# The last row of w_down in nine transfers in place of one

## The chip, the cores and the metric

The kernel runs on one core of a Trainium2 chip. The metric is the device time of one execution in microseconds. Lower is better. Before the change the median of three runs is 409.6 us (409.38 to 409.67).

## The reference

One decoding step of a transformer block, one token with a hidden size of 1024, everything in bfloat16:

```python
h  = x + attention(layernorm(x), k_cache, v_cache, wq, wo)   # 32 query heads, 4 KV heads, 65536 cached positions, head size 128
h2 = h + (gelu(n @ w_gate) * (n @ w_up)) @ w_down            # n = layernorm(h), 3584 inner columns
```

The two caches are 64 MB each, the five weight matrices together some 39 MB. All of it is read once, so the program is a stream out of HBM with the arithmetic laid alongside.

## The kernel before, in words

A ring in SBUF takes the stream in pieces. First come the two halves of wq, then for each of eight steps (a KV head and a half of the positions) the keys and the values, then wo, w_gate, w_up and w_down. Nearly all loads are issued by SyncE on one hardware queue, in the order in which they are used, each as soon as its place in the ring is free. A class `Flow` writes out this order up to w_up with semaphores set by hand (its instructions all carry line 105); TensorE's part of the attention is a loop.

For the end of the program w_down (3584 x 1024) is cut by rows. Two pieces lie in the ring: `wa` has 16 weight rows for each of the 128 partitions, `wb` 8. The last four rows of each partition lie in a tensor of their own, `w_end` (128 x 4 x 1024), so that they need not wait for room. Here "row" has two meanings: a row of w_down, of 1,024 numbers and 2 KB, and the position e that it has in its partition. One position over 128 partitions is 128 rows of w_down, 256 KB.

Behind a barrier (line 568) SyncE issues four loads, the list `loads` (line 576): `wa`, `wb`, positions 0 to 2 of `w_end`, position 3 of `w_end`. Each has a semaphore of its own, `end_sem[i]`, which counts up by 16 when the whole transfer has landed (line 579 and the lines behind it). They are issued right after one another, around 377 to 379 us, while the load of w_up still runs, and stand in the queue behind it. They take part in no wait that the framework would add; TensorE waits for the semaphores itself.

TensorE's order at the end is written by hand too. When w_up has landed, it multiplies with it (line 626); DVE and ScalarE bring the inner columns into `actz`. Then TensorE waits for `wa`, multiplies its 16 positions by wide matmuls (`down_wide`, line 647), and folds the sum into the output's banks (`add_wide`, line 653). Then comes the loop at lines 664 to 668: for each of the other three loads it waits for the load's semaphore and does `down` for each of its positions, eight matmuls of 128 columns (line 634): 8 positions of `wb`, three of `w_end`, and the last of `w_end`. Two casts (DVE, line 670; ScalarE, line 671) round the sum, and SyncE stores 2 KB (line 672).

So the last transfer has 128 pieces of 2 KB, one for each partition, and what comes behind its landing is eight matmuls, a cast, and the store.

Of the kernel before, what the change touches and what calls it, by code (L numbers as in the profile page):

```python
# [118 lines left out]
def kernel(  # L119
# [13 lines left out]
    nc = tc.nc  # L133
    P = 128
# [80 lines left out]
    end_sem = [tc.alloc_semaphore("end_landed_%d" % i) for i in range(4)]  # L215
# [40 lines left out]
    def select(key, out, op_, fill, base, pattern, mult, rows=None):  # L256
# [14 lines left out]
       in_=ident_f[:].rearrange("p (q m) -> p q m", q=4).unsqueeze(2).to_broadcast([P, 4, NI, SQ]))  # L271
# [285 lines left out]
    def ffn_load(wmat, s0):  # L557
        rk = ["R%d" % s0, "R%d" % (s0 + 1)]
        wv = slot(s0, 2)[:, 0:DC * F].rearrange("p (c n) -> p c n", c=DC)
        f.dma("sp", wv, wmat.rearrange("(p c) n -> p c n", p=P), w=rk, sem=r_sem[s0], wait=[(s_step, STEPS * NT2 - 1)])  # L560
        return wv, rk
# [5 lines left out]
    up_w, _ = ffn_load(B_w_up, 2)  # L567
    with tc.tile_critical(no_gpsimd_drain=True):  # L568
# [6 lines left out]
    FM = FB - FZ  # L575
    loads = [(wa, B_w_down[0:P * FA, :].rearrange("(p e) n -> p e n", p=P)), (wb[:, 0:FM, :], wb_src[:, 0:FM, :]),
             (w_end[:, 0:FZ - 1, :], wb_src[:, FM:FB - 1, :]), (w_end[:, FZ - 1:FZ, :], wb_src[:, FB - 1:FB, :])]
    for (dst, src), sem in zip(loads, end_sem):
        d = nc.sync.dma_start(out=dst, in_=src)  # L579
        d.then_inc(sem, 16)  # L580
        tc.no_tile_sem_insts.add(d.ins.name)
        tc.add_to_no_dep_group("loads", d.ins)
        tc.keep_in_program_order(d)
    waits_itself = nc.tensor.nop()
    tc.declare_fence(waits_itself.ins, group="loads")

# [44 lines left out]
    def down(a_row, w_row):  # L631
        for j in (0, 4, 1, 5, 2, 6, 3, 7):
            q, m = divmod(orow[j], 32)
            nc.tensor.matmul((d_ps, d_odd)[q // 2][32 * q:32 * q + 32, :], lhsT=a_row[:, AZ - m:AZ - m + 32], rhs=w_row[:, j * OB:(j + 1) * OB],  # L634
                             start=False, stop=False, skip_group_check=True, tile_position=(0, 32 * q))
# [25 lines left out]
    stay_busy(2)  # L661
    add_wide()
    e = FA
    for (dst, _), sem in list(zip(loads, end_sem))[1:]:
        nc.tensor.wait_ge(sem, 16)
        for i in range(dst.shape[1]):
            down(actz[:, e, :], dst[:, i, :])
            e += 1
# [34 lines left out]
```

## Time and profile before

| | |
|---|---|
| median of the runs | 409.6 us |
| time of the profiled execution | 409.33 us |
| its span, first to last instruction | 407.6 us |
| DMA queue of SyncE and its loads, share of 16 engines | 98.5% |
| mean rate of the DMA engines | 425 GB/s |
| TensorE, DVE, ScalarE busy | 57%, 49%, 10% |
| issue of the last load | 378.77 us |
| its landing | 404.72 us |
| issue of the store | 405.46 us |

The share of busy time is over the whole span. The end is read from stretches of a few tenths of a microsecond: there the DMA share, times 16, is the number of DMA engines that still move data.

The names in the views: `ring<-in_B_w_down_dram` are the loads `wa` and `wb`, `w_end<-in_B_w_down_dram` the two loads of `w_end`. "SPq" is SyncE's queue of issues. In a line of the timeline stand the start, the time from the first to the last of the group, the engine, line and operation, the number of instructions, and in brackets the idle time before the group with what ended it. In a line of stretches stand the stretch and its length, the busy time of TensorE, its weight loads, DVE, ScalarE and GpSimd (with the number of instructions), the granted clock of TensorE, the DMA share and the rate in GB/s.

### The profile page before, as it was taken

The page shows a single profiled execution, that of the slowest core. Times are in us where ns is not written, and L with a number is a line of the kernel's source. Part 1 is how long each engine was busy: PE and PEld are TensorE (multiplying, and loading weights), DVE is VectorE, ACT ScalarE, POOL GpSimd, SP SyncE. Part 2 cuts the span into 40 slices and gives each one's busy share as a digit, 9 for nine tenths or more (in the row PEclk, how much of TensorE's full clock was granted, in tenths as well). Part 3 has the DMA queues.
Part 4 walks back from the last instruction along what each step waited for, and adds up shares of the span by engine and source line. Part 5 has one row for each costly group of instructions (what it writes and reads, how often), then busy time and mean ns, then how long its engine had stood idle before and what let it go on. Part 6 is the DMA issues. An engine that isn't in the chain of part 4 may idle for free. (4 is left out here: it accounts for less than half of the span.)

```text
span 407.6 us, 3706 instructions
## 1 busy us (share of the span) xinstructions
PE 231.4 (57%) x1556; PEld 102.6 (25%) x1557; DVE 200.8 (49%) x160; ACT 40.0 (10%) x142; POOL 16.7 (4%) x27
## 2 busy tenths in 40 slices
PE   0432854584577368717971785468466746625366
PEld 0110322231232133203321332223123223222323
DVE  2226860875089328734763686089508940110310
ACT  1000003000300220030003000300030013000000
POOL 4210000001000000010000001000000000000200
PEclk9955996799589778976796889589956986865668
DMA  8999999999999999999998999999999999999995
GB/s 360 412 447 426 428 447 412 460 418 421 445 460 418 412 432 482 418 412 418 482 431 386 444 424 447 418 466 412 415 450 466 418 408 418 464 445 429 402 412 224
DMA packets 4958, 173.10 MB, mean 425 GB/s; under 512 B 596, under 2 KB 600, under 8 KB 856
## 3 DMA queue, kind: packets, MB, share of 16 engines
q1 hardware_dynamic: 4904, 173.02, 98.5%
q8 instruction: 4, 0.07, 0.1%
q14 instruction: 2, 0.02, 0.0%
q10 hardware_dynamic: 48, 0.00, 0.0%
HBM read 173.02 MB, written 0.00 MB: 424 GB/s over the span
## 5 line engine op out<-in xcount | busy, mean ns | idle before, releaser
L105 DVE STREAM_TRANSPOSE ktb<-ring 128x4096 f32<-128x4096 f32 x32 | 141.1, 4417 | 73.9 <-DMA ring<-in_A_k_cache_dram 73.9
L450 PE MATMUL bank<-ktb,qs 128*128 128x512 bf16 x512 | 131.4, 416 | 53.5 <-PEq L436 53.5
L450 PEld LDWEIGHTS bank<-ktb,qs 128*128 128x128 bf16 x512 | 51.4, 103 | 130.3 <-issue 84.1
L462 PE MATMUL bank<-ring,pt 128*32 128x512 bf16 x512 | 44.3, 522 | 36.6 <-PEq L436 36.6
L105 ACT ACTIVATE pt<-sc,nb 128x256 bf16<-128x256 f32 x64 | 31.5, 494 | 257.6 <-DVE nb L105 257.6
L105 DVE STREAM_TRANSPOSE sc<-bank 128x512 f32<-128x512 f32 x32 | 22.2, 695 | 37.8 <-PE bank L450 37.8
L462 PEld LDWEIGHTS bank<-ring,pt 128*32 128x32 bf16 x512 | 18.7, 126 | 59.0 <-issue 55.1
L105 PE MATMUL bank<-ring,xz 128*32 128x512 bf16 (+1 forms) x128 | 13.2, 598 | 16.8 <-DMA ring<-in_B_w_gate_dram 9.9
L105 DVE TENSOR_REDUCE mx<-sc 128x8 f32<-128x2048 f32 x8 | 18.3, 2286 | 0.3
L454 PE MATMUL bank<-ident_f,mx 128*8 128x128 f32 x8 | 2.7, 333 | 25.8 <-PEq L436 25.8
L105 POOL COPY qs<-qsel 128x512 bf16<-128x512 bf16 x4 | 5.3, 1326 | 232.7 <-PE bank L450 218.7
L105 ACT ACTIVATION_READ_ACCUMULATOR pt<-sc,nb 128x1 f32 x64 | 12.0, 187 | 0.0
L471 PE MATMUL bank<-sel,acc_sb 128*128 128x8 f32 x64 | 8.2, 255 | 6.2 <-PEq L436 6.2
L105 PEld LDWEIGHTS bank<-ring,xz 128*32 128x32 bf16 x128 | 4.8, 139 | 23.8 <-issue 14.9
L471 PEld LDWEIGHTS bank<-sel,acc_sb 128*128 128x128 f32 x64 | 7.7, 191 | 10.0 <-issue 10.0
L105 ACT COPY acc_sb<-bank 128x512 f32<-128x512 f32 x8 | 4.7, 585 | 47.0 <-PE bank L462 47.0
L626 PE MATMUL bank<-ring,xz 128*32 128x512 bf16 (+1 forms) x64 | 5.8, 556 | 4.9 <-PEq L621 4.9
L454 PEld LDWEIGHTS bank<-ident_f,mx 128*8 128x8 f32 x8 | 0.7, 83 | 29.5 <-issue 29.5
L607 DVE MEMSET bank<- 128x128 f32 x1 | 0.2, 165 | 15.2 <-SPq L568 15.2
L603 DVE STREAM_TRANSPOSE ktb<-bank 128x512 f32<-128x512 f32 (+1 forms) x4 | 2.3, 618 | 10.3 <-PE bank L626 10.3
L456 PE MATMUL bank<-diag,ones_f 8*128 8x8 f32 x16 | 3.9, 312 | 5.7 <-PEq L436 5.7
L105 DVE STREAM_TRANSPOSE ktb<-bank 128x512 f32<-128x512 f32 x2 | 1.4, 716 | 11.2 <-PE bank L105 11.1
(101 smaller groups left out, 76.5 us busy)
## 6 DMA issues: line engine op xcount, KB each, us to landing
ring<-in_A_k_cache_dram SPq DMA_DIRECT2D x16, 4096.0 KB, 24.8
ring<-in_A_wq_dram SPq DMA_DIRECT2D x2, 4096.0 KB, 16.6
ring<-in_A_wo_dram SPq DMA_DIRECT2D x2, 4096.0 KB, 24.1
ring<-in_B_w_gate_dram SPq DMA_DIRECT2D x1, 7168.0 KB, 26.1
ring<-in_B_w_up_dram SPq DMA_DIRECT2D x1, 7168.0 KB, 31.8
ring<-in_B_w_down_dram SPq DMA_DIRECT2D x1, 4096.0 KB, 20.2
ring<-in_B_w_down_dram SPq DMA_DIRECT2D x1, 2048.0 KB, 24.7
w_end<-in_B_w_down_dram SPq DMA_DIRECT2D x1, 768.0 KB, 25.8
```

What stands on the lines that cost most here:

```text
L105: ins = getattr(self.eng[e], o["call"])(**o["kw"])
L450: m = nc.tensor.matmul(bank[c][:], lhsT=qs[:, jt].rearrange("p s c -> p (s c)")[:, s * P:(s + 1) * P], rhs=mv[:, :, J, :, u], start=(s == ...
L454: nc.tensor.transpose(out=mxT_ps, in_=mx1[:], identity=ident_f[:]).then_inc(s_step, 1)
L456: nc.tensor.matmul(bc_ps, lhsT=ones_f[0:rep, :], rhs=diag[:], start=True, stop=True).then_inc(s_step, 1)
L462: m = nc.tensor.matmul(acc[32 * q:32 * q + 32, :], lhsT=pt[:, c, n, :, :].rearrange("p h s -> p (h s)"), rhs=v_sb[:, c, :, n, :], start=(c ...
L471: m = nc.tensor.matmul(o_ps, lhsT=acc_sb[:, u * Dh:(u + 1) * Dh], rhs=sel[:, u:SQ:NS], start=(u == 0), stop=(u == NS - 1))
L603: nc.vector.transpose(out=r[:, o:o + n].rearrange("p (e j) -> p e j", j=32), in_=ps.rearrange("p (j e) -> p e j", j=32))
L607: nc.vector.memset(d_ps, 0.0)
L626: nc.tensor.matmul(f_banks[t // 4][32 * q:32 * q + 32, :], lhsT=hz[:, ci, :], rhs=w, start=(ci == 0), stop=(ci == DC - 1), tile_position=( ...
```

## The change

The last load, position 3 of `w_end`, is issued as nine transfers by partitions: the first 64, then 1, 3, 5, 7, 9, 11, 13 and 15. Together they are the same 128 pieces of 2 KB from the same places to the same places. All nine count up the same semaphore, and TensorE waits for 9 x 16 = 144 in place of 16. The other three loads, their order and the matmuls stay.

```diff
-    for (dst, src), sem in zip(loads, end_sem):
-        d = nc.sync.dma_start(out=dst, in_=src)
-        d.then_inc(sem, 16)
-        tc.no_tile_sem_insts.add(d.ins.name)
-        tc.add_to_no_dep_group("loads", d.ins)
-        tc.keep_in_program_order(d)
+    stairs, p0 = [], 0
+    for n in [P // 2] + list(range(1, 16, 2)):
+        stairs.append(slice(p0, p0 + n))
+        p0 += n
+    assert p0 == P
+    shares = [[slice(0, P)]] * 3 + [stairs]
+    for (dst, src), sem, share in zip(loads, end_sem, shares):
+        for p in share:
+            d = nc.sync.dma_start(out=dst[p], in_=src[p])
+            d.then_inc(sem, 16)
+            tc.no_tile_sem_insts.add(d.ins.name)
+            tc.add_to_no_dep_group("loads", d.ins)
+            tc.keep_in_program_order(d)
...
-    for (dst, _), sem in list(zip(loads, end_sem))[1:]:
-        nc.tensor.wait_ge(sem, 16)
+    for (dst, _), sem, share in list(zip(loads, end_sem, shares))[1:]:
+        nc.tensor.wait_ge(sem, 16 * len(share))
         for i in range(dst.shape[1]):
```

## The prediction

> **What bounds the kernel now.** I read the page first: the slices and the queues of its parts 2 and 3, then the chain that ended last, then stretches of the last microseconds, the timeline there, and the waits of SyncE.
>
> ```profile
> DMA  8999999999999999999998999999999999999995
> DMA packets 4958, 173.10 MB, mean 425 GB/s; under 512 B 596, under 2 KB 600, under 8 KB 856
> q1 hardware_dynamic: 4904, 173.02, 98.5%
> q8 instruction: 4, 0.07, 0.1%
> q14 instruction: 2, 0.02, 0.0%
> ```
>
> The 16 DMA engines are busy from the first slice to the last but one, 98.5% of the span with loads alone: the kernel is a stream of 173 MB, and it ends when the last byte of w_down is in and used. Programs are fetched through the same engines (q8, q14).
>
> ```profile
> 378.77 25.95 DMA w_end<-in_B_w_down_dram
> 404.72 0.04 issue
> 404.76 0.35 PE bank L634 x8
> 405.12 0.02 issue
> 405.14 0.26 ACT h L671
> ```
>
> The chain in order of time (start, duration): the transfer that the change cuts up is the last load on it. Its issue is at 378.77, but it stands in the queue for most of its 25.95 us; what sets the end is when the slowest engine finishes its part.
>
> ```profile
> 401.60:401.80 0.20, 0.20 (x4) 0.20 (x6) 0.00 (x0) 0.00 (x0) 0.00 (x0) 1.00 1.05 430
> 402.60:402.80 0.20, 0.20 (x28) 0.20 (x20) 0.00 (x0) 0.00 (x0) 0.00 (x0) 1.00 0.56 205
> 403.20:403.40 0.20, 0.18 (x16) 0.00 (x1) 0.00 (x0) 0.00 (x0) 0.00 (x0) 1.00 0.23 92
> 403.60:403.80 0.20, 0.00 (x0) 0.00 (x0) 0.00 (x0) 0.00 (x0) 0.00 (x0) 1.00 0.25 92
> 404.00:404.20 0.20, 0.06 (x4) 0.06 (x8) 0.00 (x0) 0.00 (x0) 0.00 (x0) 1.00 0.16 61
> ```
>
> Stretches of 0.2 us (engines' busy time, granted clock, DMA share, GB/s). The DMA share falls from 1.05 to 0.23: from 403.2 on, about four of sixteen engines still work. The stream doesn't end at once; it drains over two microseconds.
>
> ```profile
> 404.14 0.34 PEld L634 LDWEIGHTS <-ktb 128*32 128x32 bf16 x24 [0.94 <-DMA w_end<-in_B_w_down_dram]
> 404.76 0.12 PEld L634 LDWEIGHTS <-ktb 128*32 128x32 bf16 x8 [0.28 <-DMA w_end<-in_B_w_down_dram]
> SPq L672 <- DVE h L670: 26.2, 1, 26.2
> ```
>
> TensorE multiplies the three rows of the third transfer at 404.14, stands idle for 0.28 us, and takes the last row. SyncE, which issues the loads, has nothing else for 26.2 us.
>
> **Which engines are late.** The trace has every DMA packet's start and duration. On each engine a packet starts where the one before ended, so they fall into sixteen chains, all of which process the same sequence. Behind the first to finish, the sixteen end the last transfer at 0, 0.12, 0.26, 0.27, 0.29, 0.31, 0.35, 0.37, 0.45, 0.49, and then 0.93, 1.37, 1.69, 1.84, 1.96 and 1.98 us. The lags are old: they stay for hundreds of microseconds, since no engine ever runs dry. Each of the six late ones got its lag at a program fetch on that engine: 16,384 bytes at 31.9, 353.9, 376.9 and 401.0 us cost some 1.5 us each, 8,192 bytes at 103.2 and 144.3 us 1.0 and 0.7. The records do not give an engine's number.
>
> **The change, part by part.**
>
> *The shares.* Now every engine has 8 packets of 2,048 bytes in the last transfer, 80 ns each by the records, 0.64 us, and one 6 ns mark that counts up the semaphore. After: 64 rows over sixteen engines, 4 packets each; then eight transfers of 1 to 15 rows. How many engines a small transfer uses is shown twice: the x load of 32 rows left two packets and a mark on each of sixteen, and the output store of 4 rows left 4 packets and 4 marks. I take the nearest, the store: n rows, n engines, one packet each. If the eight always begin at the same engine, the shares are 12, 11, 11, 10, 10, 9, 9, 8, 8, 7, 7, 6, 6, 5, 5 and 4 packets (sum 128, as before), with up to 8 further marks: from +0.32 + 0.05 = +0.37 us for the first engine to -0.32 us for the last. If they rotate, each keeps 8 packets, +0.02 us on average for marks. The Trainium skill, "DMA: Bandwidth & Descriptors", section "Why a DMA increments its semaphore by 16 and not by 1", says that a transfer takes the largest count up to 16 that divides its rows, on the lowest-numbered engines. By that rule the shares are the graded ones; the store's four marks agree, and no row shows an odd count.
>
> *Which shares the late engines get.* This is what decides, and nothing in the trace tells. Bounds: all three of the latest (1.84, 1.96, 1.98) at the light end, where the end would come up to 0.3 us sooner, or the latest on the first engine, +0.37. Each of the sixteen orders being as likely, I drew the sixteen shares at random over the sixteen lags: the latest of lag plus share is in the middle +0.17 us, one time in ten below -0.01, one in ten above +0.35, and only one time in ten is it a gain. That is because three engines lie within 0.15 us, two packets, and the worst share among them counts. The ten early engines have 1.49 us (1.98 - 0.49) to spare, more than any share takes. I take +0.17.
>
> *What a gain is cut by.* If the last row lands sooner, TensorE is still at the three rows before it, which come over the same late engines and are not changed. The 0.28 us of idle time in the row above is all that can be had.
>
> *Issues.* SyncE issues twelve loads in place of four. The two issues to w_end took 0.43 us each, so eight more are 8 x 0.43 = 3.4 us: from 379.2 to 382.6. The first of these rows is wanted by the engines at some 402.4, 20 us later, and behind them on SyncE is only the store at 405.46, under the 26.2 us. Costed at nothing; were the cover gone it would be 3.4 us. No other engine waits for SyncE after its barrier at 377.1, and nothing on ACT's queue or POOL's is moved.
>
> *The wait.* TensorE's wait is for 144 in place of 16, still one instruction. Behind it are the last 8 matmuls, then the two casts and the store, as before: 0.
>
> *TensorE's work* is the same 96 matmuls on the same tiles: 0.
>
> Sum, against the profiled execution's own time of 409.33 us (span 407.6 and 1.7 outside): 409.33 + 0.17 = 409.5. The median of the runs is 409.6, 0.27 above that execution, so 409.6 + 0.17 = 409.8.
>
> **The rivals.**
>
> *Light shares for the late engines.* Were the late engines late because they stand at the end that the small transfers skip, the gain is 0.15 to 0.28 us: 409.3 to 409.5. For it: four of the six carry the same kind of fetch, so they may be neighbours. Against it: neighbours in the middle or at the front are as likely.
>
> *Writers in each other's way.* Today every transfer of the stream goes to all 128 rows at once, and the steady 80 ns shows no conflict. Now sixteen engines write within the first 64 rows, and then within the last 64; if two that share a way into SBUF halve their rate, the packets of the late four go from 80 to up to 160 ns. Over 8 packets that is +0.64, with the +0.17 some +0.3 to +0.85 us: 409.9 to 410.45. Against it: when the late four drain, the other twelve are done, and the four are 0.3 us apart. The Trainium skill, "SBUF — State Buffer", section "Door 1: The DMA port swizzle", has 64 adjoining rows on only 8 of 16 ports, which speaks against this change; no run here shows it, and by it the sum would be this rival's.
>
> *A fetch more.* Eight more instructions may push SyncE's program over the edge of a block. The 8 KB fetches cost their engine 0.7 and 1.0 us; it counts in full only on one of the three latest: 410.3 to 410.6. Against it: ten of sixteen engines have 1.49 us to spare.
>
> *Slower: the odd transfers go to one engine.* If a count that isn't a power of two isn't spread, one engine has 4 + 64 = 68 packets in place of 8: 60 x 0.08 = 4.8 us more. On an engine as late as the latest the end moves by 4.8, on the earliest by 4.8 - 1.98 = 2.8: 412.4 to 414.4. It decides from 25 packets (1.98 / 0.08) on an early engine, from any on a late one. For it: no row shows an odd count; the rows shown are 128, 32 and 4. Against it: the 4.
>
> **How the numbers follow.** Forecast 0.62; light shares 0.12; writers in the way 0.12, a third of which passes 0.2%; a fetch 0.04, half of it; one engine 0.08; 0.02 for what I have not seen, put to faster. 0.2% (0.8 us) is about what a measurement of this kernel can tell from no change; no share of the staircase moves it by that. Same: 0.62 + 0.12 + 0.08 + 0.02 = 0.84; slower 0.04 + 0.02 + 0.08 = 0.14; faster 0.02. The range goes from 409.3 (light shares in full) to 410.5 (writers in the way), leaving the one-engine case and part of the fetch out, 0.1 to 0.15 in all.
>
> **What would show it.** The queue's packet count should rise by 8 transfers' marks, 64, the bytes staying. Stretches of 0.2 us from 402.4 should show the early ten engines drain more unevenly and about four busy up to 404.2. The landing of the last of w_end at 404.6 to 405.1, and TensorE's idle time before its last 8 matmuls between 0 and 0.65 us in place of 0.28. SyncE: twelve issues, the last ended near 382.6. Wrong would be: a long single-engine tail (DMA share 0.06 for microseconds), packets of 2 KB well over 80 ns, a third q14 packet, or lags that don't come from the fetches.

## The result and the profile after

The changed kernel takes 410.39 us (median of ten runs, 410.29 to 410.79), beside 409.40 us for the kernel before. The ratio is 1.0024, with a 95% interval of 1.0015 to 1.0034: a loss of about 1.0 us. The profiled execution took 410.39 us, with a span of 408.7.

The page of the changed kernel, its slices and queues:

```profile
DMA  8999999999999999999999998999999999999994
DMA packets 5022, 173.10 MB, mean 424 GB/s; under 512 B 660, under 2 KB 664, under 8 KB 920
q1 hardware_dynamic: 4968, 173.02, 98.4%
q8 instruction: 4, 0.07, 0.1%
q14 instruction: 2, 0.02, 0.0%
```

The stream is the same 173.10 MB with 64 packets more, the marks of the eight added transfers (a mark is the 4-byte packet by which an engine counts up the semaphore; a transfer of n rows left n of them, and 1 + 3 + ... + 15 is 64). No program fetch was added. The chain that ended last, in order of time:

```profile
381.60 0.35 SPq L586
381.94 0.04 issue
381.98 23.81 DMA w_end<-in_B_w_down_dram
405.79 0.04 issue
405.83 0.35 PE bank L641 x8
406.19 0.02 issue
406.21 0.26 ACT h L678
```

The landing moved from 404.72 to 405.79, +1.07 us, and what comes behind it is as before: 0.04, 0.35, 0.02. (The first line is the eleventh of twelve issues; the twelfth starts at 381.98, where the DMA line starts, and ends at 382.35.) So the whole loss lies ahead of the landing. Some stretches ahead of it, the first from the kernel before, the others from the changed one (stretch, length, busy times of the engines, clock, DMA share, GB/s):

```profile
402.40:402.60 0.20, 0.20 (x23) 0.20 (x24) 0.00 (x0) 0.00 (x0) 0.00 (x0) 1.00 0.81 318
```

```profile
402.40:402.60 0.20, 0.20 (x20) 0.20 (x24) 0.00 (x0) 0.00 (x0) 0.00 (x0) 1.00 0.89 184
402.60:402.80 0.20, 0.20 (x29) 0.20 (x21) 0.00 (x0) 0.00 (x0) 0.00 (x0) 1.00 0.82 164
...
404.60:404.80 0.20, 0.00 (x0) 0.00 (x0) 0.00 (x0) 0.00 (x0) 0.00 (x0) 1.00 0.09 31
404.80:405.00 0.20, 0.02 (x4) 0.03 (x7) 0.00 (x0) 0.00 (x0) 0.00 (x0) 1.00 0.00 0
405.00:406.00 1.00, 0.66 (x32) 0.44 (x32) 0.00 (x0) 0.00 (x0) 0.00 (x0) 1.00 0.00 0
```

Two things are to be seen. From 402.4 to 402.8 more engines are busy than before and move less; in the first of these stretches a busy engine moves about half as much: 318 / (0.81 x 16) = 24.5 GB/s before, 184 / (0.89 x 16) = 12.9 after. And from 404.8 no DMA engine has anything to do, but the transfer lands at 405.79, one microsecond later. TensorE's timeline shows the same gaps:

```profile
404.98 0.34 PEld L641 LDWEIGHTS <-ktb 128*32 128x32 bf16 x24 [1.73 <-DMA w_end<-in_B_w_down_dram]
405.83 0.12 PEld L641 LDWEIGHTS <-ktb 128*32 128x32 bf16 x8 [0.51 <-DMA w_end<-in_B_w_down_dram]
```

The three positions of the third transfer come 0.84 us later than before (404.14), though that transfer wasn't changed, and the last position waits 0.51 us in place of 0.28.

The records of single packets tell where. Of two late engines in the changed kernel (bytes of a packet and its duration in ns, M where a mark was written, in us):

```
6144:239 6144:234 6144:234 6144:324 6144:452 6144:475 6144:258 6144:234 M404.007
   2048:84 x4 M404.332  2048:84 M404.418  2048:84 M404.504  2048:84 M404.590
   2048:84 M404.676  2048:84 M404.762
... 6144:351 6144:412 6144:292 6144:432 6144:339 6144:275 M404.391
   2048:86 2048:85 2048:84 2048:84 M404.721  2048:84 M404.807
```

Their 6 KB packets took 235 ns before and up to 475 now, while the early engines were at their single rows, whose 2 KB packets took mostly 110 to 175 ns. The last packet of all ended at 404.81, in the kernel before at 404.29: +0.52 us. And the six marks that the first of these engines wrote 86 ns apart, from 404.332 on, reached the semaphore at 404.811, 405.007, 405.203, 405.399, 405.595 and 405.791: 196 ns apart. (The records of landings don't name the engine; these six are taken for its marks by their number and their even steps, here and below.) So from the last packet to the landing it is 0.98 us, in place of 0.43: +0.55. Together +1.07.

Two theories came out of this, beside that of the prediction (graded shares): **conflict** of engines that write a few adjoining rows at once, and **late marks**, an engine's marks passing one after another at a fixed pace. A string of marks is such a row: each is written before the one ahead of it has landed.

### The profile page after: what moved, and what is told of

Its sections match the earlier page's. It is cut to its first block, busy times and chain, and to the rows that moved or that the text cites. A ratio compares the mean times of both kernels' runs of the same rounds, so it can differ in the third digit from the quotient of the medians.

```text
span 408.7 us, 3714 instructions
## 1 busy us (share of the span) xinstructions
PE 227.1 (56%) x1556; PEld 101.6 (25%) x1557; DVE 200.8 (49%) x160; ACT 40.0 (10%) x142; POOL 16.7 (4%) x27
## 2 busy tenths in 40 slices
DMA packets 5022, 173.10 MB, mean 424 GB/s; under 512 B 660, under 2 KB 664, under 8 KB 920
## 5 line engine op out<-in xcount | busy, mean ns | idle before, releaser
L462 PE MATMUL bank<-ring,pt 128*32 128x512 bf16 x512 | 42.4, 504 | 36.5 <-PEq L436 36.5
L105 PE MATMUL bank<-ring,ktb 128*32 128x512 bf16 x64 | 6.1, 545 | 2.7 <-DMA ring<-in_A_wo_dram 2.0
```

Source lines behind the costliest of these rows:

```text
L105: ins = getattr(self.eng[e], o["call"])(**o["kw"])
L462: m = nc.tensor.matmul(acc[32 * q:32 * q + 32, :], lhsT=pt[:, c, n, :, :].rearrange("p h s -> p (h s)"), rhs=v_sb[:, c, :, n, :], start=(c ...
```

## The experiments

Each is compared with the kernel before on the same chip, whose median there was 409.34 us (two halves, 8 tiny on one semaphore, 64 rows last, eight of 16) or 409.35 us (the other four). Each edit is against the changed kernel.

| kernel | us | ratio, 95% interval | last packet ended | landing | between |
|---|---|---|---|---|---|
| before | 409.4 | | 404.29 | 404.72 | 0.43 |
| the change | 410.39 | 1.0024 (1.0015 to 1.0034) | 404.81 | 405.79 | 0.98 |
| two halves | 410.0 | 1.0015 (1.0006 to 1.0024) | 404.91 | 405.32 | 0.41 |
| even and odd rows | 409.39 | 1.0001 (0.9992 to 1.001) | 404.18 | 404.59 | 0.41 |
| uncut, 4 tiny behind | 409.99 | 1.0018 (1.0009 to 1.0027) | 404.36 | 405.34 | 0.98 |
| uncut, 8 tiny behind | 410.68 | 1.003 (1.0019 to 1.0041) | 404.44 | 406.09 | 1.65 |
| the same, own semaphores | 410.94 | 1.0038 (1.0024 to 1.0051) | 404.52 | 406.25 | 1.73 |
| 64 rows last | 410.49 | 1.0027 (1.0017 to 1.0038) | 404.87 | 405.90 | 1.03 |
| eight of 16 adjoining rows | 410.79 | 1.0035 (1.0021 to 1.0049) | 404.87 | 406.08 | 1.21 |
| the change, rows spread | 410.25 | 1.002 (1.0011 to 1.0029) | 404.29 | 405.43 | 1.14 |

(The last three columns are from one profiled execution of each: the packet and semaphore records. "Last packet" includes its mark.)

**Two halves.**

```diff
-    stairs, p0 = [], 0
...
+    stairs = [slice(0, P // 2), slice(P // 2, P)]
```

> The last load as two transfers, the first 64 rows and the last 64: equal shares of 8 packets on every engine, two marks per engine with 4 packets between them. Before: 409.4 us, the change: 410.4. If the loss comes from many engines writing within half of the rows, most of the conflict is here too: the late engines' 6,144-byte packets go from 235 to 280 to 480 ns, and the time to 409.9 to 410.1. If the conflict needs transfers of a few adjoining rows, packets stay at 84 and 235 ns and the time within 0.1 us of before. If the loss comes from strings of marks, 409.4: two marks 0.33 us apart make no string. If it comes from graded shares, 409.4.

410.0 us: 0.66 us lost with equal shares and without a string of marks. The stretch and the landing of this kernel:

```profile
402.40:402.60 0.20, 0.20 (x20) 0.20 (x24) 0.00 (x0) 0.00 (x0) 0.00 (x0) 1.00 0.89 174
...
404.80:405.00 0.20, 0.17 (x12) 0.17 (x16) 0.00 (x0) 0.00 (x0) 0.00 (x0) 1.00 0.03 10
```

```profile
404.83 0.35 PEld L637 LDWEIGHTS <-ktb 128*32 128x32 bf16 x24 [1.61 <-DMA w_end<-in_B_w_down_dram]
405.36 0.12 PEld L637 LDWEIGHTS <-ktb 128*32 128x32 bf16 x8 [0.19 <-DMA w_end<-in_B_w_down_dram]
```

The busy engines are as slow as in the change (174 GB/s at a share of 0.89), and the bytes end 0.62 us late; the landing follows them by 0.41 as before. In the records the late engines' 6 KB packets go up to 489 ns, and the early engines' second four packets of 2 KB take 124 to 207 ns. Their first four stay at 84. So there is a loss with lengthened packets and without a string of marks, at the size that the first case named; that it comes from the place of the rows, and not from having two transfers, is for the next run to show.

**Even and odd rows**, the same two transfers with other rows.

```diff
+    stairs = [slice(0, P, 2), slice(1, P, 2)]
```

> The last load as two transfers of 64 rows again, but the even rows and then the odd rows in place of the first half and the second. Count of transfers, shares and marks are those of the two adjoining halves (410.0 us beside 409.34 before). If the loss there comes from where the rows lie, every packet stays at 84 and 235 ns here, and the time is 409.3 to 409.5. If it comes from having two transfers on the same tensor in flight, or from the second mark, 410.0 again.

409.39 us, ratio 1.0001.

```profile
402.40:402.60 0.20, 0.20 (x28) 0.20 (x20) 0.00 (x0) 0.00 (x0) 0.00 (x0) 1.00 0.69 256
```

```profile
404.63 0.12 PEld L637 LDWEIGHTS <-ktb 128*32 128x32 bf16 x8 [0.28 <-DMA w_end<-in_B_w_down_dram]
```

A busy engine moves 23 GB/s here (256 / 11.0), every packet of the late engines stays at 84 and 234 ns, but for the two at a program fetch, of 654 and 369 ns (as before), and the idle time before the last eight matmuls is the 0.28 us of the kernel before. Where the rows lie is the whole of the 0.66 us; a second transfer and a second mark cost nothing that can be measured. The Trainium skill, "SBUF — State Buffer", section "Door 1: The DMA port swizzle", has 64 adjoining rows on 8 of 16 ports, and by its formula the even rows are on all of them; this pair of runs agrees, 410.0 beside 409.39 us. But the even and odd rows lie elsewhere in HBM too, so the runs don't tell whether it is the writes to SBUF or the reads from HBM that get in each other's way; that it is the writes is argued, from the ports that the Trainium skill gives, and not shown.

**Eight tiny transfers behind an uncut last load.**

```diff
+    stairs = [slice(0, P)]
...
+    for i in range(NTINY):   # 8
+        d = nc.sync.dma_start(out=tiny[:, i, :], in_=B_w_down[i, 0:512].rearrange("(p n) -> p n", p=16))
+        d.then_inc(end_sem[3], 16)
...
-        nc.tensor.wait_ge(sem, 16 * len(share))
+        nc.tensor.wait_ge(sem, 16 * (len(share) + (NTINY if sem is end_sem[3] else 0)))
```

> The last load stays one transfer of 128 rows, and eight transfers of 16 pieces of 64 bytes are issued behind it on the same semaphore, so that every engine has nine marks in place of one and hardly more bytes (8 x 64 B, some 17 ns for a piece and its mark). If an engine's marks reach the semaphore only some 0.2 us after one another, however fast they are written, the landing comes 8 x 0.18 = 1.4 us later, with no DMA packet running in that time: 410.8 to 411.0. If marks cost what the packet records show (6 to 9 ns), 8 x 0.02 = 0.16 us: 409.6. The conflict of writers and the graded shares have no part in this kernel: 409.6 by them.

410.68 us, just under what late marks were given. The stretches and TensorE's timeline:

```profile
404.40:404.60 0.20, 0.20 (x24) 0.11 (x9) 0.00 (x0) 0.00 (x0) 0.00 (x0) 1.00 0.02 1
404.60:404.80 0.20, 0.09 (x8) 0.00 (x0) 0.00 (x0) 0.00 (x0) 0.00 (x0) 1.00 0.00 0
404.80:405.00 0.20, 0.00 (x0) 0.00 (x0) 0.00 (x0) 0.00 (x0) 0.00 (x0) 1.00 0.00 0
405.00:406.00 1.00, 0.00 (x0) 0.00 (x0) 0.00 (x0) 0.00 (x0) 0.00 (x0) 1.00 0.00 0
```

```profile
404.17 0.52 PE L645 MATMUL bank<-w_end,ktb 128*32 128x128 bf16 x24 [0.78 <-DMA w_end<-in_B_w_down_dram]
406.13 0.30 PE L645 MATMUL bank<-w_end,ktb 128*32 128x128 bf16 x8 [1.44 <-DMA tiny<-in_B_w_down_dram]
```

Nothing runs on the whole core for over a microsecond: the bytes are there, the third transfer came as early as before, and TensorE waits 1.44 us for marks alone. In the packet records a piece of 64 bytes and its mark take 13 ns; in the time it is 1.34 / 8 = 0.17 us each. That is an average: the last landings are a string of nine, from 404.521 to 406.089, each 0.196 us behind the one before, as in the change. Other strings of nine in this trace have steps of 0.151, 0.159, 0.177 and 0.203 us, each nearly the same from mark to mark. Late marks are shown without conflict: no packet is lengthened, but for the two at a program fetch.

**Four of them.**

```diff
-    NTINY = 8
+    NTINY = 4
```

> As the kernel with eight tiny transfers behind an uncut last load, with four of them. If marks pass one after another at a fixed pace, the loss is half: 1.34 / 2 = 0.67 us, 410.0, with the landing 0.17 to 0.2 us later for each. If the loss is a fixed price for having tiny transfers there, 410.7 again.

409.99 us, 0.64 us lost: half, as a fixed pace has it, 0.16 us each.

```profile
405.38 0.30 PE L645 MATMUL bank<-w_end,ktb 128*32 128x128 bf16 x8 [0.72 <-DMA tiny<-in_B_w_down_dram]
```

TensorE's wait is half too, 0.72 us beside 1.44. With four the string that lands last is another, five marks in steps of 0.152 us up to 405.340; one with steps of 0.196 ends at 405.253.

**Eight with a semaphore each.**

```diff
-        d.then_inc(end_sem[3], 16)
+        d.then_inc(tiny_sem[i], 16)
...
+        if sem is end_sem[3]:
+            for x in tiny_sem:
+                nc.tensor.wait_ge(x, 16)
```

> As the kernel with eight tiny transfers, but each of the eight has a semaphore of its own, and TensorE waits for all of them. If the pace is that of one semaphore counted up by all engines, each semaphore now gets 16 marks in place of 144 and most of the 1.34 us goes: 409.5 to 409.7. If the pace is that of one engine, which lets a mark out only when the one before is in, 410.7 as with the shared semaphore.

410.94 us, nothing won. The pace is not that of one semaphore that all engines count up; it is that of the marks of one engine. With a semaphore for each transfer the strings can be followed from one to the next: the last landings on them lie, for one engine, 0.197 to 0.214 us apart (404.623 to 406.247, the end), for another 0.158 to 0.169 (404.863 to 406.175). The 0.26 us over the shared semaphore is explained in part: the profiled execution shows 0.14 us between the landing and the matmuls (0.04 before), behind eight waits in place of one, and its bytes ended 0.08 us later.

**64 rows last.**

```diff
+    stairs = stairs[1:] + stairs[:1]
```

> The same nine transfers, with the 64 rows issued last in place of first: same shares, same rows, same count of marks, but each engine's last mark stands behind 4 packets (0.34 us). If strings of marks make the landing late, half or more of the 0.55 us between the last packet and the landing goes: 409.9 to 410.1. If that time has another cause, or the whole loss is conflict and shares, 410.4 as the change.

410.49 us, where late marks were given 409.9 to 410.1: a miss, and its cause is in my arithmetic. The four packets ahead of the last mark take 0.33 us, but the mark itself needs its 0.2 us, so that they make up only some 0.13. And what is won at the end is lost at the start. The engine's first small mark now stands right behind its mark of the third transfer, 404.195 behind 404.109, and lands 0.72 us after it was written; in the change the first mark behind the third transfer's, that of the 64 rows, stood behind four packets (404.332 behind 404.007), and it took 0.48. The records show the string unbroken: the last marks of the slowest engine were written at 404.367, 404.453, 404.539 and, behind the four packets, 404.865, and the last four landings are at 405.310, 405.506, 405.701 and 405.897, still 196 ns apart. In both orders the string begins with the mark of the third transfer, and the last landing is 1.20 us behind that mark's (404.589 to 405.791 in the change, 404.701 to 405.897 here). The order in which the transfers are issued saves nothing.

**Eight transfers of 16 adjoining rows.**

```diff
+    stairs = [slice(i, i + 16) for i in range(0, P, 16)]
```

> The last load as eight transfers of 16 adjoining rows: every engine has 8 packets as before, and 8 marks. If engines that write a few adjoining rows at once get in each other's way, the 2 KB packets go from 84 to 110 to 170 ns and the late engines' 6,144-byte packets beside them to 280 to 480, +0.6 us; if strings of marks cost, 7 more marks some 0.11 us each, +0.8; both together 410.6 to 411.0. With the marks alone 410.2, with the conflict alone 410.0. By graded shares alone 409.4 to 409.5, since here the shares are equal.

410.79 us: both costs. Bytes end 0.58 us late, the 6 KB packets go up to 479 ns, and from the last packet to the landing it is 1.21 us. The packets between the marks are of 2 KB, and strings of eight landings have steps of 0.158 us (ending at 406.005), 0.196 (ending at 406.077, the last) and 0.203: the pace differs from string to string, as with the tiny pieces, and doesn't go with the size of the packet. Shares are equal here, and it is slower than the change; graded shares are not what costs.

**The change with its rows spread.**

```diff
+    stairs, p0 = [slice(0, P, 2)], 1
+    for n in range(1, 16, 2):
+        stairs.append(slice(p0, min(p0 + 2 * n, P), 2))
+        p0 += 2 * n
```

> The change with its rows spread: the 64 even rows, and 1, 3, 5 up to 15 of the odd rows, each with one row left out between neighbours. Counts, shares and marks are those of the change, so its 0.5 us of late marks stays. If the other 0.5 us is conflict over adjoining rows, some half of it or more goes: 409.9 to 410.2. If the place of the rows is nothing, 410.35 as the change.

410.25 us, just above what conflict was given. The bytes end at 404.29, where they ended before the change, and the third transfer is used at 404.45 in place of 404.98:

```profile
404.45 0.52 PE L641 MATMUL bank<-w_end,ktb 128*32 128x128 bf16 x24 [1.06 <-DMA w_end<-in_B_w_down_dram]
405.47 0.30 PE L641 MATMUL bank<-w_end,ktb 128*32 128x128 bf16 x8 [0.50 <-DMA w_end<-in_B_w_down_dram]
```

Nearly all the delay of the bytes is gone (the 6 KB packets still go up to 336 ns), but only 0.14 us of the time (the profiled execution, the fastest of the eleven at 410.04, shows more, 0.35). The bound has moved to an engine with a longer string: one wrote seven marks from 403.748 to 404.264, and at 0.43 us for the first and 0.196 for each further it should land at 404.18 + 6 x 0.196 = 405.35; the landing was at 405.43. So the two costs don't simply add: conflict with hardly any string costs 0.66 us (the halves), the strings with most of the conflict gone 0.90, and both together 1.0. A staircase without its strings of marks was not run.

None of these beats the kernel before. The best that the staircase could have won, by its shares, was 0.28 us, less than two marks cost.

## Why the prediction was right or wrong

The range held the time (410.39 in 409.3 to 410.5), but the point, 409.8, was 0.6 us low: a loss of 0.17 us was forecast, and 0.99 was measured. The chance of 0.84 was on "within 0.2%"; the measured 0.24% is just over it, with the bound inside its interval (0.15 to 0.34). That the range held is luck in part. Its upper end was made for conflict of writers alone; the loss is that conflict and late marks together, and the shares, which made up the forecast, were not what cost.

- **What bounds the end** was right: the late engines set it, their lags come from program fetches (in the changed kernel again the same six fetches, four of 16 KB and two of 8 KB), and everything behind the landing kept its durations.
- **The shares** were read rightly. In the records one engine writes eight single packets behind its four, others fewer, down to none; odd counts do spread, so the slower rival, one engine for all of an odd transfer, fell. The rule of the lowest-numbered engines that the prediction takes from the Trainium skill fits this; the records give no engine's number, so the numbers themselves are not shown. But the shares didn't decide: of the two engines that ended last one had a light share (5 packets) and one 9, and the one with 9 landed last, because it had the longer string of marks. The graded shares by themselves were not measured; in the staircase with its rows spread, which has the same shares, the bytes ended at 404.29 us, as with equal shares before the change.
- **"One 6 ns mark"** is the step that failed. The 6 to 9 ns are what a mark takes in the packet records; as a price of being waited for it is 0.15 to 0.21 us for each mark behind another of the same engine, behind tiny packets and 2 KB ones alike, and 0.196 on the string that ended the change. With five marks behind the first on that engine, 5 x (0.196 - 0.086) = 0.55 us: as much as the longer time from the last packet to the landing. I had costed up to 8 marks at 0.05 us. The Trainium skill, "DMA: Bandwidth & Descriptors", section "Queues, rings and completion order", says that a semaphore increment lands only after all earlier writes of its engine; that would make marks late, and I didn't weigh it. The Trainium skill, the same page, section "Anatomy of one DMA — SWDGE (gpsimd) path", which is about transfers that GpSimd issues, calls the semaphore write essentially free, about one cycle, and puts most of a transfer's fixed cost down to the receipt of the data. For SyncE's transfers here the measurement decides, and it is 0.15 us and more where marks follow one another.
- **"Writers in each other's way"**, given 0.12, is the other half. Its size came out, up to +0.64 for the conflict alone against the measured 0.66 of the halves, but by luck: the 0.64 was worked out for other packets. It was added up from the late engines' last eight 2 KB packets at half their rate, and the argument against it was about the same packets: when the others are done, these do stay at 84 ns. The harm is done earlier: while the early engines write adjoining rows, the late ones are still at the 6 KB packets of the transfer before, and these take up to twice as long. One of the signs that the prediction named for being wrong was there: the early engines' 2 KB packets at 110 to 175 ns.
- **Bounds on the landing** (404.6 to 405.1) fell with it: 405.79. The idle time before the last matmuls, 0.51 us, was inside 0 to 0.65, because the third transfer came late as well.
- **Issues**: 8 more were to take 3.4 us and end near 382.6; they end at 382.35, far ahead of use. **A fetch more** didn't come: q14 still has two packets. **Light shares** as a gain were not seen.

## What to carry to other kernels

A transfer cut into small ones behind one another is paid for in completions: in these runs each engine's marks arrive only 0.15 to 0.2 us apart, so the number of transfers that end a queue counts, not their bytes. And rows that are written at once should be spread over all partitions; here 64 adjoining ones slowed even the transfer ahead of them, 64 alternate ones cost nothing. To read it in a profile, look for stretches with a high DMA share and few GB/s (conflict), and for a landing long after the DMA share has gone to zero (marks).

## What the runs showed that I had not expected

- Marks written 13 ns apart (64-byte pieces) and marks written 86 ns apart (2 KB) are passed on at the same steps, 0.15 to 0.21 us, nearly constant within a string and different from string to string; eight semaphores in place of one don't help. That speaks for a fixed time for each mark and against one that goes with the bytes before it, but what a mark waits for, and why the strings differ, is not shown.
- In the first half of the rows the early engines' four packets stayed at 84 ns; the lengthening (124 to 207 ns) began with the second half. That writes are held in a buffer at first would fit, but it was not tried.
- A late engine's lag of up to 2 us, most of it got at a program fetch up to 370 us earlier, is still there at the end, in every trace of this case.
